# Four tiles in place of two for each step of an expert layer, and a new order of the steps behind the last loads

## The chip, the cores and the metric

The kernel runs on one core of one Trainium2 chip. The metric is the time of one execution in device microseconds. Before the change three runs took 282.29, 282.82 and 283.61 us, the median is 282.82 us.

## The reference

An attention over 49 agents per batch is followed by a soft mixture of experts. Everything is float32, and there are B = 4 batches of N = 11456 tokens with C = 128 channels.

```
a2k  = softmax(scale * agents @ k.T)        agent_v = a2k @ v
q2a  = softmax(scale * q @ agents.T)        x = q2a @ agent_v        (45824 x 128)
logits = x @ phi                            (45824 x 32: 8 experts with 4 slots each)
d = softmax(logits, over the tokens)        slot_input = d.T @ x
slot_out[e] = max(slot_input[e] @ w1[e], 0) @ w2[e]                  (F = 1024)
c = softmax(logits, over the slots)         out = c @ slot_out       (45824 x 128)
```

## The kernel before

The tokens of a batch lie in 90 cells of 128 (four streams of 32), so there are 360 cells. The program is a list of 1281 small steps, each with one engine, the steps that it depends on, and the buffer slots that it takes and gives back. A table of names, `ORDER` (line 49), fixes one order for all of them; each engine then works its own steps off strictly in that order, and the loads and stores are all issued from SP's queue in that order too. The framework adds the semaphore waits, by tile.

The work comes in three stages. The first reads k, v and q in groups of 16 cells, makes the scores on TensorE (`ks`, `qs`, line 243), the softmaxes on VectorE, ScalarE and GpSimd, and the sums of the experts' inputs (`rg`, lines 590 and 598). `x_all` keeps the logits of all cells for the end.

The second stage is the expert layer, between the last sum and the first output. `l4` (line 801) writes the slots' inputs `si`. The hidden layer of 1024 is cut into four quarters, numbered by `fh` (0, 1) and `q` (0, 1). Each quarter is multiplied by w1 (`mh`, line 828, 8 matmuls that the trace shows as 16), rectified (`mr`, line 834 on VectorE for q = 0, line 837 on ScalarE for q = 1), transposed (`mt`, line 844), copied (`mc`, line 848 on ScalarE for q = 0, line 850 on VectorE for q = 1) and multiplied by w2 (`mo`, line 857). The four `mo` add up in one PSUM tile `so_p`; then follow the copy `ms` (line 863), the sum over experts `sb` (868), and `sd` (871), which scales by the tokens' divisor `dr` (`d2` to `d4`, lines 810 to 820) and gives `sob`. Before the change the two quarters of one `fh` share one tile at each step: `hp`, `hs`, `htp` and `ht` have a dimension of two, and each quarter uses its half:

```python
hps[fh] = tile_("s", [P, 2, 512], f"hp_{fh}")      # PSUM, one of three slots "s"
v_.tensor_scalar(out=hss[fh][:, 0, :256], in0=hps[fh][:, 0, :256], ...)      # q = 0
s_.activation(out=hss[fh][:, 1, :256], in_=hps[fh][:, 1, :256], func=AF.Relu)   # q = 1
```

The third stage makes the output in 25 chunks of 4, 4, 8, 8 and then 16 cells. For the cells of each group it takes the logits' maximum (`cr`, line 607, VectorE), subtracts it (`cu`, 611, GpSimd) and takes the exponential (`ce`, 616, ScalarE); for each chunk j it then makes the sum `os` (875, VectorE), the small addition `oe` (879, ScalarE), the reciprocal `or` (882, VectorE), the product `om` (887, GpSimd), the transpose `ot` (893, VectorE), the matmuls with `sob` (`oo`, 901, TensorE, two PSUM buffers), and two copies out of PSUM into one of four output buffers: `va` (911, VectorE, a quarter) and `vb` (914, ScalarE, three quarters). `od` (918) stores it from SP's queue. The steps from `cr` to `ot` can be done long before `sob` is there; where they stand is up to the table. `oo` of chunk 0 is the first that needs `sob`.

The weights are eight loads of 1 MB, `w1` (705) and `w2` (710). `w2` with x = 1, 2, 3 goes into the buffers of q (`qt`), the others into a pool that opens when the last groups of k are done (`ends`, line 925).

Of the kernel before, what the change touches and what calls it, by code (L numbers as in the profile page):

```python
# [100 lines left out]
r412 qv10 ru9.0 re9.0 ru9.1 cu14 r312 rx12 ql11 os1 eh ei qM11 r211 r411 w12 re9.1 ry12.0 r311 or0
cu8 om0 nm os6 rx11 rg9.0 rg12.0 rc12 wt rg9.1 rc9 wr oe1 ry11.0 rg11.0 ry11.1 rg11.1 ws gm qv11
ce10 rc11 l1 l2 w10 f0 ce14 f1 f2 os2 ce11 cu13 l3 l4 oe6 cr19 os4 oe4 dE or1 mh0.0 or3 ot0 mh0.1
mr0.0 om1 cu12 ot1 qv12 w13 mh1.0 os12 os5 mr1.0 cr18 ej mr0.1 ce8 ce12 oe2 om3 mt0.0 mt0.1 mc0.1
mh1.1 mc0.0 mo0 ce15 oe12 mt1.0 or12 or6 oe5 w21 mo1 os7 oe8 or4 os16 or2 cu19 w23 mr1.1 mt1.1
mc1.1 or5 om5 om2 mc1.0 d1 d2 oe7 cr22 cu18 mo2 mo3 ms d3 d4 os13 or7 ce18 oe13 cu22 sb sd oo0 oo1
or8 os17 va0 vb0 om8 od0 ot2 oo2 ot3 ce13 ce17 va1 vb1 od1 os10 va2 om4 vb2 or13 ot4 oo3 va3 om13
om7 om6 vb3 oe10 od3 ot5 cr20 od2 oo4 va4 oo5 ot6 os14 ce19 vb4 od4 ot7 va5 or10 cu20 oe14 cr23
oe9 or9 cu23 om9 vb5 od5 oo6 oo7 va6 ot8 ot9 ce20 os11 vb6 od6 oe11 va7 os15 oe15 or15 om10 oo8
vb7 od7 or14 or11 va8 ot10 om11 oe17 os19 os18 os20 vb8 oo9 va9 oe19 ot11 or19 od8 vb9 od9 om12  # L110
ot12 oo10 va10 vb10 cr21 or17 cr24 cu21 oe16 od10 oo11 va11 ce21 oe20 os22 vb11 od11 om19 ot13
om14 or16 oo12 ot14 oe22 om15 om17 va12 vb12 od12 oo13 oo14 va13 vb13 od13 ot15 va14 oe18 or18
om16 ot16 oo15 ot17 cu24 ce24 vb14 or20 oo16 va15 vb15 od14 om18 ot18 ot19 om20 va16 ot20 ce22
oo17 va17 vb16 od15 vb17 od17 os21 oe21 os23 or22 om22 oo18 va18 vb18 od18 or21 oe23 or23 ce23
os24 oe24 or24 om23 oo19 va19 vb19 od16 od19 oo20 va20 vb20 od20 om21 ot21 oo21 ot22 oo22 ot23
va21 vb21 od21 va22 vb22 od22 oo23 va23 vb23 od23 om24 ot24 oo24 va24 vb24 od24
# [980 lines left out]
```

## Time and profile before

| | |
|---|---|
| runs shown | 282.29, 282.82, 283.61 us (median 282.82) |
| the profiled execution | 284.2 us |
| its span from first to last instruction | 282.3 us |
| busy in the span: TensorE, VectorE, ScalarE, GpSimd | 87%, 78%, 70%, 45% |
| HBM read, written | 79.73 MB, 23.59 MB |
| output stores | 25, of which 21 have 1024 KB |

Times in the profile count from the span's start. "DVE" is VectorE, "ACT" ScalarE, "POOL" GpSimd, "PE" TensorE's matmuls and "PEld" its weight loads, "SPq" the queue from which SyncE issues the transfers. Line numbers are those of the kernel before. A time in square brackets is how long the engine had been idle before the row, with the instruction that ended the wait.

### The profile page before, as it was taken

What the parts mean: (1) busy time and instruction counts of PE and PEld (TensorE: products, weight loads), DVE (VectorE), ACT (ScalarE), POOL (GpSimd) and SP (SyncE); (2) the same over time, 40 slices, a digit from 0 to 9 for tenths busy, and PEclk for the clock granted to TensorE, in tenths of its full rate; (3) what the DMA queues carried; (4) which work ended last, traced back from release to release, by engine and by line L of the source; (5) the groups of instructions that cost most, each with busy time, mean ns of one, the idle gap of its engine ahead of it and who ended that gap; (6) DMA issues with size and microseconds to landing.
All of it is one profiled execution on the core that took longest, in us unless ns stands there. A gap on an engine that the chain in (4) does not pass through costs nothing.

```text
span 282.3 us, 8243 instructions
## 1 busy us (share of the span) xinstructions
PE 244.4 (87%) x3252; PEld 131.4 (47%) x3252; DVE 220.6 (78%) x431; ACT 198.7 (70%) x680; POOL 126.3 (45%) x139
## 2 busy tenths in 40 slices
PE   7959889999999989999999999999987699596810
PEld 4213556642554654455674555777744323131300
DVE  0597774699998977999898999999676999676520
ACT  2559597466997876599798978997643767866540
POOL 0034521207565341474754485994645834725000
PEclk9999999999999999999999999999799987957575
DMA  7999999999999999999999999559900499999995
GB/s 252 425 424 416 419 410 414 423 412 418 346 416 422 416 420 417 407 366 415 419 418 419 421 376 424 201 201 421 414 14 0 193 416 406 411 425 416 423 417 245
DMA packets 16454, 103.86 MB, mean 368 GB/s; under 512 B 2080, under 2 KB 2464, under 8 KB 5152
## 3 DMA queue, kind: packets, MB, share of 16 engines
q1 hardware_dynamic: 16272, 103.25, 89.9%
q8 instruction: 26, 0.43, 0.6%
q10 hardware_dynamic: 144, 0.08, 0.1%
q14 instruction: 12, 0.10, 0.1%
HBM read 79.73 MB, written 23.59 MB: 366 GB/s over the span
## 4 chain that ended last, share of the span: by engine, by line
PE 46%; DMA 32%; DVE 9%; ACT 4%; issue 2%; POOL 2%; SPq 1%; ACTq 0%; DVEq 0%
DMA out<-ot 11%; PE sq L243 11%; PE sk L243 9%; DMA vt<-vL 9%; PE ev L320 8%; DMA kt<-kT 7%; DMA qt<-qT 6%; PE tp L477 5%; PE lq L528 4%; ACT ot L914 3%; PE gp L598 2%; DVE cd L875 2%; PE gp L590 2%; POOL x_all L887 1%; PE so_p L857 1%
## 5 line engine op out<-in xcount | busy, mean ns | idle before, releaser
L445 ACT ACTIVATE pt<-pt,mx 128x49 f32<-128x49 f32 x148 | 47.5, 326 | 0.1
L320 PE MATMUL ev<-vt,et 128*64 128x129 f32 x720 | 44.8, 276 | 3.1 <-DMA vt<-vL 2.7
L243 PE MATMUL sk<-kt,ag 128*32 128x512 f32 (+1 forms) x384 | 45.7, 570 | 1.4 <-DMA kt<-kT 1.1
L243 PE MATMUL sq<-qt,ag 128*32 128x512 f32 (+3 forms) x400 | 43.8, 554 | 3.2 <-DMA qt<-qT 3.0
L320 PEld LDWEIGHTS ev<-vt,et 128*64 128x64 f32 x720 | 39.2, 136 | 10.0 <-issue 6.2
L901 PE MATMUL pa<-ct,sob 32*128 32x512 f32 (+2 forms) x50 | 32.1, 750 | 12.1 <-DVE ct L893 10.1
L466 POOL TENSOR_TENSOR pt<-pt,rt 128x784 f32<-128x784 f32 (+3 forms) x20 | 27.1, 1356 | 33.5 <-DVE rt L462 25.4
L914 ACT COPY ot<-pb 128x1536 f32<-128x1536 f32 (+2 forms) x25 | 32.5, 1306 | 12.7 <-DMA out<-ot 8.1
L303 ACT ACTIVATE es<-sk,nm 128x512 f32<-128x512 f32 (+1 forms) x48 | 29.7, 652 | 10.1 <-DVE nm L294 8.2
L564 POOL TENSOR_TENSOR dt<-x_all,mb 128x512 f32<-128x512 f32 (+1 forms) x20 | 24.2, 1218 | 22.6 <-DVE mb L560 15.1
L887 POOL TENSOR_TENSOR x_all<-x_all,cd 128x512 f32<-128x512 f32 (+2 forms) x25 | 23.5, 961 | 23.1 <-DVE cd L882 18.1
L901 PE MATMUL pb<-ct,sob 32*128 32x512 f32 (+2 forms) x150 | 33.6, 772 | 0.1
L313 DVE STREAM_TRANSPOSE et<-es 128x1024 f32<-128x1024 f32 (+1 forms) x24 | 28.0, 1165 | 3.1 <-ACT es L303 3.1
L611 POOL TENSOR_TENSOR x_all<-x_all,r_all 128x512 f32<-128x512 f32 (+3 forms) x25 | 23.9, 962 | 11.7 <-DVE r_all L607 5.9
L482 ACT COPY pT<-tp 128x1024 f32<-128x1024 f32 (+3 forms) x25 | 22.8, 918 | 8.6 <-PE tp L477 8.6
L275 DVE TENSOR_REDUCE mt<-sk 128x2 f32<-128x1024 f32 (+1 forms) x24 | 27.4, 1140 | 1.8 <-PE sk L243 1.5
L445 ACT ACTIVATION_READ_ACCUMULATOR pt<-pt,mx 128x1 f32 x148 | 28.1, 190 | 0.0
L911 DVE COPY ot<-pa 128x512 f32<-128x512 f32 (+2 forms) x25 | 15.5, 620 | 11.2 <-DMA out<-ot 9.2
L901 PEld LDWEIGHTS pa<-ct,sob 32*128 32x128 f32 x50 | 9.3, 226 | 31.9 <-DVE ct L893 20.2
L420 DVE STREAM_TRANSPOSE pt<-sq 128x1024 f32<-128x1024 f32 (+3 forms) x20 | 21.8, 1095 | 2.0 <-PE sq L243 1.5
L243 PEld LDWEIGHTS sq<-qt,ag 128*32 128x32 f32 x400 | 11.0, 109 | 22.9 <-issue 16.3
L477 PE MATMUL tp<-cs,pt 128*128 128x128 f32 x140 | 21.4, 283 | 0.0
(133 smaller groups left out, 421.4 us busy)
## 6 DMA issues: line engine op xcount, KB each, us to landing
out<-ot SPq DMA_DIRECT2D x21, 1024.0 KB, 7.7
vt<-vL SPq DMA_DIRECT2D x20, 1032.0 KB, 11.5
qt<-qT SPq DMA_DIRECT2D x20, 1024.0 KB, 9.6
kt<-kT SPq DMA_DIRECT2D x19, 1024.0 KB, 9.4
w2s<-w SPq DMA_DIRECT2D x4, 1024.0 KB, 13.5
w1s<-w SPq DMA_DIRECT2D x4, 1024.0 KB, 11.2
vt<-vL SPq DMA_DIRECT2D x4, 645.0 KB, 8.6
kt<-kT SPq DMA_DIRECT2D x4, 640.0 KB, 9.0
```

What stands on the lines that cost most here:

```text
L243: t_.matmul(sp[32 * q4:32 * q4 + 32, h, :nt], ag[:, b, 32 * h:32 * h + 32], xv[:, q4, :], start=True, stop=True)
L275: v_.tensor_reduce(out=k["mt"][:, 0:2], in_=k["s"][:, :, :nt], axis=AX.X, op=ALU.max, negate=True)
L303: s_.activation(out=k["e"][:, h, :nt], in_=k["s"][:, h, :nt], func=AF.Exp, bias=k["nm"][:, 2 * h:2 * h + 1])
L313: v_.transpose(out=k["et"][:, :n].rearrange("p t (h a) -> p h t a", h=2), in_=k["e"][:, :, :nt].rearrange("p h (t a) -> p h t a", a=32))
L320: t_.matmul(k["ev"][o:o + AW, :], k["et"][:, c, :], k["v"][:, c, :], start=c < 2, stop=c >= n - 2)
L445: s_.activation(out=x, in_=x, func=AF.Exp, bias=q["mx"][:, c:c + 1], accum_out=q["rt"][:, c:c + 1])
L466: g_.tensor_tensor(out=x, in0=x, op=ALU.mult, in1=q["rt"][:, :n].unsqueeze(2).to_broadcast([P, n, A]))
L477: t_.transpose(q["tp"][:, h, j % 4, :], q["pt"][:, 2 * j:2 * j + 2, :].rearrange("p c a -> p (c a)"), ident)
L564: g_.tensor_tensor(out=q["dt"][:, :q["n"]], in0=x_all[:, q["at"]:q["at"] + q["n"]], op=ALU.add, in1=r["mb"].unsqueeze(1).to_broadcast([P, ...
L887: g_.tensor_tensor(out=x, in0=x, op=ALU.mult, in1=z["cd", j].unsqueeze(2).to_broadcast([P, n, S]))
L901: t_.matmul(pb[:, r - 1, :32 * n] if r else pa[:, :32 * n], sob[32 * r:32 * r + 32, :], z["ct", j][32 * r:32 * r + 32, :32 * n], start=Tru ...
L914: s_.copy(out=o_ov(j)[:, 1:4], in_=z["pb", j][:, :, :32 * CHUNKS[j]])
```

## The change

Each quarter of the expert layer gets tiles of its own: `hp` and `htp` (PSUM) and `hs` and `ht` (SBUF) are made once for each `fh` and `q`. The steps lose their dependence on the other quarter of the same `fh`, the slots are taken where the tile is written and given back when that one tile is done with, and `mc` takes its own SBUF slot. The first output matmul gets the last transposes of the logits (`qv`) as a further dependence. The table `ORDER` is new from the end of the last k groups on: the same 1281 steps stand in another order there, loads included. No operation is added, and none is removed.

```diff
-qc21 cu16 kv22 kE22 kv23 cu11 kE23 cr14 cr17 cu7 qw24 ka22 qE22.3 ce16 qr24 qr19 ce7 cr15 qr23
+qc21 cu16 kv22 kE22 kv23 cu11 cr14 cu7 qr19 qN19 cr15 kE23 cr12 w21 qE22.3 ka22 qr23 kA22 ce4 kA23
...
     def m_h(fh, q):
-        if q == 0:
-            hps[fh] = tile_("s", [P, 2, 512], f"hp_{fh}")
-            hss[fh] = tile_("pt", [P, 2, 512], f"hs_{fh}")
+        h = hps[fh, q] = tile_("s", [P, 256], f"hp_{fh}{q}")
...
     def m_relu(fh, q):
-        if q == 0:
-            v_.tensor_scalar(out=hss[fh][:, 0, :256], in0=hps[fh][:, 0, :256], scalar1=0.0,
-                             scalar2=None, op0=ALU.max)
+        h = hss[fh, q] = tile_("pt", [P, 256], f"hs_{fh}{q}")
+        if q:
+            s_.activation(out=h, in_=hps[fh, q], func=AF.Relu)
         else:
-            s_.activation(out=hss[fh][:, 1, :256], in_=hps[fh][:, 1, :256], func=AF.Relu)
+            v_.tensor_scalar(out=h, in0=hps[fh, q], scalar1=0.0, scalar2=None, op0=ALU.max)
 
     def m_trans(fh, q):
-        if q == 0:
-            htp[fh] = tile_("s", [P, 2, 4, P], f"htp_{fh}")
-            hts[fh] = tile_("pt", [P, 2, 4, P], f"ht_{fh}")
+        htp[fh, q] = tile_("s", [P, 2, P], f"htp_{fh}{q}")
...
     def m_copy(fh, q):
-        if q == 0:
-            s_.copy(out=hts[fh][:, 0, 0:2], in_=htp[fh][:, 0, 0:2])
+        h = hts[fh, q] = tile_("pt", [P, 2, P], f"ht_{fh}{q}")
+        if q:
+            v_.tensor_copy(out=h, in_=htp[fh, q])
         else:
-            v_.tensor_copy(out=hts[fh][:, 1, 0:2], in_=htp[fh][:, 1, 0:2])
+            s_.copy(out=h, in_=htp[fh, q])
...
+            h = op("mh", (fh, q), "P", lambda fh=fh, q=q: m_h(fh, q),
+                   deps=[si4] + wx[2 * fh:2 * fh + 2], takes=("s",))
+            r = op("mr", (fh, q), "A" if q else "V", lambda fh=fh, q=q: m_relu(fh, q),
+                   deps=(h,), takes=("pt",), gives=(("s", h),))
+            t = op("mt", (fh, q), "P", lambda fh=fh, q=q: m_trans(fh, q), deps=(r,),
+                   takes=("s",), gives=(("pt", r),))
+            c[2 * fh + q] = op("mc", (fh, q), "V" if q else "A", lambda fh=fh, q=q: m_copy(fh, q),
+                               deps=(t,), takes=("pt",), gives=(("s", t),))
...
+    ops["oo", 0]["deps"] += [("qv", ri) for ri in range(NR)]
```

Three places in the order of the instructions show what moves. The first is ScalarE in the expert layer. The steps `mr` (line 837 before, 833 now) and `mc` (848, 847) stand among the exponentials and the small additions; in square brackets is the engine whose semaphore the instruction waits for. Before:

```order
L879 ACTIVATE cd_3090<-cd_3090 128x16 [waits DVE_49]
L837 ACTIVATE hs_3099<-hp_3098 128x256 [waits DVE_49]
L616 ACTIVATE x_all<-x_all 128x512 [waits Pool_49] x2
L879 ACTIVATE cd_3081<-cd_3081 128x8
L848 COPY ht_3149<-htp_3148 128x256 [waits DVE_49]
L616 ACTIVATE x_all<-x_all 128x512
...
L837 ACTIVATE hs_3127<-hp_3126 128x256 [waits PE_49]
L848 COPY ht_3176<-htp_3175 128x256 [waits DVE_49]
```

And with the change:

```order
L876 ACTIVATE cd_3100<-cd_3100 128x16 [waits DVE_49]
L833 ACTIVATE hs_3133<-hp_3124 128x256 [waits PE_49]
L833 ACTIVATE hs_3146<-hp_3137 128x256 [waits PE_49]
L847 COPY ht_3151<-htp_3148 128x256 [waits PE_49]
L616 ACTIVATE x_all<-x_all 128x512
...
L847 COPY ht_3213<-htp_3188 128x256 [waits PE_49]
L616 ACTIVATE x_all<-x_all 128x512
L616 ACTIVATE x_all<-x_all 128x512 [waits Pool_49]
L820 COPY dr<-dr_p 128x1 [waits PE_49]
```

Three of the four instructions waited for VectorE, which had its own half of the same tile to write or read; now all four wait for TensorE alone.

The second place is TensorE in the expert layer (line 826 now was 828, 840 was 844, 854 was 857). Before:

```order
L828 MATMUL hp_3126<-w1s,si 32x256 [waits DMAHW6_49]
L828 MATMUL hp_3126<-w1s,si 32x256 x3
L844 MATMUL htp_3148<-cs,hs_3099 128x128 [waits DVE_49]
L844 MATMUL htp_3148<-cs,hs_3099 128x128
L844 MATMUL htp_3148<-cs,hs_3099 128x128 [waits Activation_49]
L844 MATMUL htp_3148<-cs,hs_3099 128x128
L828 MATMUL hp_3126<-w1s,si 32x256 [waits DVE_49]
L828 MATMUL hp_3126<-w1s,si 32x256 x7
L857 MATMUL so_p<-w2s_2825,ht_3149 32x256 [waits DMAHW2_49,Activation_49]
```

And with the change:

```order
L826 MATMUL hp_3137<-w1s,si 32x256 x3
L840 MATMUL htp_3148<-cs,hs_3116 128x128 [waits DVE_49]
L840 MATMUL htp_3148<-cs,hs_3116 128x128
L751 MATMUL d_p<-cs,gt 32x1
L826 MATMUL hp_3159<-w1s,si 32x256 [waits Activation_49]
L826 MATMUL hp_3159<-w1s,si 32x256 x7
L840 MATMUL htp_3168<-cs,hs_3133 128x128 [waits Activation_49]
L840 MATMUL htp_3168<-cs,hs_3133 128x128
L840 MATMUL htp_3171<-cs,hs_3146 128x128 [waits Activation_49]
L840 MATMUL htp_3171<-cs,hs_3146 128x128
L854 MATMUL so_p<-w2s_2801,ht_3151 32x256 [waits DMAHW7_49,DVE_49]
```

Three products stand ahead of the first transpose in both; the fourth stood behind a wait for VectorE (the half of its own tile that VectorE reads) and now stands behind one transpose and a wait for ScalarE (a PSUM slot given back), and two transposes separate it from the first product with w2.

The third place is VectorE between the copies `va` of chunks 0 and 3 (line 911 before, 908 now). Before:

```order
L911 COPY ot_3273<-pa_3258 128x128
L893 STREAM_TRANSPOSE ct_3278<-x_all 128x256
L893 STREAM_TRANSPOSE ct_3286<-x_all 128x256
L911 COPY ot_3290<-pa_3264 128x128
L875 TENSOR_REDUCE cd_3294<-x_all 128x16
L911 COPY ot_3296<-pa_3280 128x256
L882 RECIPROCAL cd_3238<-cd_3238 128x16
L893 STREAM_TRANSPOSE ct_3301<-x_all 128x512
L911 COPY ot_3309<-pa_3303 128x256
```

And with the change:

```order
L908 COPY ot_3274<-pa_3268 128x128
L890 STREAM_TRANSPOSE ct_3276<-x_all 128x256
L879 RECIPROCAL cd_3079<-cd_3079 128x16
L879 RECIPROCAL cd_3100<-cd_3100 128x16
L908 COPY ot_3291<-pa_3283 128x128
L879 RECIPROCAL cd_2816<-cd_2816 128x16
L890 STREAM_TRANSPOSE ct_3310<-x_all 128x512
L908 COPY ot_3312<-pa_3298 128x256
L890 STREAM_TRANSPOSE ct_3314<-x_all 128x512
L607 TENSOR_REDUCE r_all<-x_all 128x4
L879 RECIPROCAL cd_3233<-cd_3233 128x16
L607 TENSOR_REDUCE r_all<-x_all 128x16
```

One transpose has gone ahead of `sob`, and so has the reduction between the copies of chunks 1 and 2; three reciprocals have come between. On SP's queue the load of `w2` with x = 1, which stood behind the wait for the last k groups, stands ahead of it now, directly behind the last load of v, and needs no wait; six loads of weights are left behind the wait where seven were.

## Rows read from the trace of the kernel before

**Rows 1.** Stretches: us, busy PE, PEld, DVE, ACT, POOL, granted clock, DMA share, GB/s.
```profile
180.00:185.00 5.00, 5.00 (x86) 4.63 (x84) 4.77 (x11) 4.71 (x15) 4.54 (x5) 1.00 0.18 70
...
220.00:225.00 5.00, 3.96 (x32) 1.53 (x32) 4.48 (x12) 4.83 (x9) 4.38 (x6) 1.00 0.53 205
225.00:230.00 5.00, 3.72 (x21) 1.50 (x24) 4.68 (x11) 3.51 (x6) 3.05 (x4) 1.00 1.04 421
230.00:235.00 5.00, 4.90 (x17) 1.50 (x15) 4.72 (x12) 3.32 (x6) 2.33 (x3) 0.51 0.95 392
```
**Rows 2.** Timeline, expert layer: start, us, engine, line, operation, count [idle <-releaser].
```profile
203.48 0.91 DVE L540 STREAM_TRANSPOSE x_all<-lq 128x704 f32<-128x704 f32 x1
205.45 0.18 DVE L801 TENSOR_TENSOR si<-si_p,sie 128x32 f32<-128x32 f32 x1
205.69 2.80 PE L828 MATMUL hp<-w1s,si 128*32 128x256 f32 x48
206.14 0.68 DVE L875 TENSOR_REDUCE cd<-x_all 128x16 f32<-128x512 f32 x1
207.69 0.42 DVE L834 TENSOR_SCALAR hs<-hp 128x256 f32<-128x256 f32 x1 [0.52 <-PE hp L828]
208.15 0.38 ACT L837 ACTIVATE hs<-hp 128x256 f32<-128x256 f32 x1 [1.07 <-DVE hs L834]
208.58 0.66 PE L844 MATMUL htp<-cs,hs 128*128 128x128 f32 x4
210.07 1.07 PE L828 MATMUL hp<-w1s,si 128*32 128x256 f32 x16 [0.83 <-DVE hs L834]
211.03 0.37 ACT L848 COPY ht<-htp 128x256 f32<-128x256 f32 x1 [1.37 <-DVE ht L850]
211.46 1.07 PE L857 MATMUL so_p<-w2s,ht 128*32 128x256 f32 x16 [0.31 <-ACT ht L848]
214.76 0.37 ACT L848 COPY ht<-htp 128x256 f32<-128x256 f32 x1 [2.24 <-DVE ht L850]
215.18 1.93 PE L857 MATMUL so_p<-w2s,ht 128*32 128x256 f32 x32 [0.77 <-ACT ht L848]
217.19 0.42 DVE L863 COPY so<-so_p 128x256 f32<-128x256 f32 x1 [1.25 <-PE so_p L857]
218.49 0.35 DVE L871 TENSOR_SCALAR sob<-sb_p,dr 128x128 f32<-128x128 f32 x1
```
**Rows 3.** Timeline, the first output chunks.
```profile
219.46 0.28 DVE L911 COPY ot<-pa 128x128 f32<-128x128 f32 x1
219.54 0.48 ACT L914 COPY ot<-pb 128x384 f32<-128x384 f32 x1 [1.09 <-PE pb L901]
219.92 0.99 ACT L616 ACTIVATE x_all<-x_all 128x512 f32<-128x512 f32 x2
221.43 0.24 DVE L882 RECIPROCAL cd<-cd 128x16 f32<-128x16 f32 x1
222.96 0.62 ACT L616 ACTIVATE x_all<-x_all 128x512 f32<-128x512 f32 x1
223.57 1.44 ACT L914 COPY ot<-pb 128x1536 f32<-128x1536 f32 x1
223.64 0.68 DVE L911 COPY ot<-pa 128x512 f32<-128x512 f32 x1
225.03 10.12 SPq L918 DMA_DIRECT2D out<-ot  x5
```
**Rows 4.** Timeline, the matmuls of two later chunks, at half clock and at full.
```profile
231.24 2.07 PE L901 MATMUL pa<-ct,sob 32*128 32x512 f32 x2
...
238.00 1.12 PE L901 MATMUL pa<-ct,sob 32*128 32x512 f32 x2
```
**Rows 5.** SP's queue: the last loads of v, the first load behind the wait.
```profile
169.66 8.24 SPq L266 DMA_DIRECT2D vt<-vL  x2
185.59 0.33 SPq L710 DMA_DIRECT2D w2s<-w  x1
```

More of the change, by code (lines that the diff above doesn't have):

```diff
@@ L101 @@
[L101 to L116, printed above, removed]
+qc21 cu16 kv22 kE22 kv23 cu11 cr14 cu7 qr19 qN19 cr15 kE23 cr12 w21 qE22.3 ka22 qr23 kA22 ce4 kA23
+w12 qw24 re8.0 eb cu8 qp18.0 qp18.1 w23 w10 qN23 kg23.1 qw22 kh23.1 qr24 os2 cr13 kg23.2 kh23.2
@@ new lines @@
+os1 qN24 kh23.4 w11 w20 qp19.0 kg23.3 os3 os6 w13 qr22 os8 kh23.3 qp19.1 ql10 qM10 r210 qc18 qc19
+oe6 ec ed qp24.0 qc24 ql9 r410 r310 ce16 oe1 qN22 qp22.0 qM9 qv9 rx10 rg8.0 r29 ry10.0 rg8.1 rc8
+qp22.1 oe2 ry10.1 cu2 ce2 qc22 ef qz24 qp23.0 eg cu15 ce7 ce15 r49 ql12 rg10.0 rg10.1 r39 or2 qM12
+r59 or1 r212 r412 qc23 ql11 ru9.0 rc10 ru9.1 qv10 r312 rx12 re9.0 eh ei qM11 r211 ry12.0 r411 r311
+nm os0 rg9.0 rg12.0 om1 re9.1 rg9.1 rx11 rc12 wt wr oe3 cr20 cu20 cu14 ce11 rc9 f0 ry11.0 rg11.0
+ry11.1 rg11.1 ws gm os5 oe0 rc11 l1 or0 qv12 om0 ce8 oe5 ce14 f1 l2 l3 oe8 cr17 f2 l4 os10 qv11 dE
@@ new lines @@
+mh0.0 mr0.0 oe10 or6 os4 os16 mh0.1 mr0.1 or3 ej mh1.1 mr1.1 mt0.0 mc0.0 ce10 os7 oe7 d1 mh1.0
+mt0.1 mt1.1 mo0 cr22 ot0 mr1.0 mt1.0 oe4 om6 cu17 mc0.1 cu13 ce13 or4 om4 om2 cr21 mc1.1 mo1 ce17
+mc1.0 mo2 mo3 ot1 os17 cu12 ce20 ce12 cr19 ot2 d2 ms os14 d3 or7 sb d4 sd om3 os9 oo0 va0 ot3 cu21
+om7 or5 om5 or10 oo1 vb0 od0 va1 oe9 vb1 or8 om8 od1 oo2 oo3 ot4 va2 ot5 cr24 oe17 om10 or17 vb2
+od2 cr18 va3 oo4 vb3 va4 ot6 ot7 od3 oo5 vb4 od4 or9 om9 cu18 os18 va5 ot8 ce21 vb5 od5 ce9 os12
+oo6 va6 os15 ce18 vb6 od6 ot9 ot10 oe12 cu22 ce22 os23 oe14 or12 om12 oo7 oo8 oe16 va7 vb7 od7 va8
@@ new lines @@
+vb8 od8 or14 om17 om14 oo9 os13 os11 oe11 or11 va9 oo10 va10 vb10 od10 oe23 os22 om11 cu19 or23
+ot11 os19 ot12 ce19 oo11 oe13 or13 om13 om23 os20 oe15 or15 vb9 va11 od9 cu24 om15 vb11 od11 ot13
+oe18 or18 om18 oe19 oo12 ot14 va12 vb12 oe20 or19 oo13 va13 or16 vb13 od13 oo14 ot15 om16 ot16
+ot17 oe22 or22 om22 va14 or20 om20 vb14 od14 oo15 va15 ot18 oo16 om19 vb15 od15 od12 oo17 va16
+vb16 va17 oo18 va18 vb17 od16 ot19 ot20 vb18 od18 oo19 os21 oe21 or21 om21 va19 vb19 ot21 cr23
+cu23 ce23 ce24 od17 oo20 oo21 va21 vb21 od21 va20 os24 oe24 vb20 od20 ot22 or24 om24 ot23 oo22
@@ L117 @@
+va22 ot24 vb22 od22 oo23 va23 od19 vb23 od23 oo24 va24 vb24 od24
 """
@@ L958, in tile_agent_attn_soft_moe @@
     d4 = op("d4", (), "A", z_d4, deps=(d3,), gives=(("a", d3),))
-    h, t, c = {}, {}, {}
+    c = {}
     for fh in range(2):
-        h[fh] = [op("mh", (fh, q), "P", lambda fh=fh, q=q: m_h(fh, q),
-                    deps=[si4] + wx[2 * fh:2 * fh + 2] + ([("mh", fh, 0)] if q else []),
-                    takes=() if q else ("s", "pt")) for q in range(2)]
-        r = [op("mr", (fh, q), "A" if q else "V", lambda fh=fh, q=q: m_relu(fh, q),
-                deps=[h[fh][q]], gives=(("s", h[fh][0]),)) for q in range(2)]
-        t[fh] = [op("mt", (fh, q), "P", lambda fh=fh, q=q: m_trans(fh, q),
-                    deps=[r[q]] + ([("mt", fh, 0)] if q else []),
-                    takes=() if q else ("s", "pt"), gives=(("pt", h[fh][0]),)) for q in range(2)]
-        c[fh] = [op("mc", (fh, q), "V" if q else "A", lambda fh=fh, q=q: m_copy(fh, q),
-                    deps=[t[fh][q]], gives=(("s", t[fh][0]),)) for q in range(2)]
+        for q in range(2):
+            h = op("mh", (fh, q), "P", lambda fh=fh, q=q: m_h(fh, q),
[6 more added lines that the diff above has]
+                               deps=(t,), takes=("pt",), gives=(("s", t),))
     mo = None
@@ L974, in tile_agent_attn_soft_moe @@
         mo = op("mo", (x,), "P", lambda x=x: m_out(x),
-                deps=[c[x // 2][x % 2], wy[x], ("am", 0)] + ([mo] if mo else []),
-                takes=() if x else ("a",), gives=(("pt", t[x // 2][0]),))
+                deps=[c[x], wy[x], ("am", 0)] + ([mo] if mo else []),
+                takes=() if x else ("a",), gives=(("pt", c[x]),))
     ms = op("ms", (), "V", m_so, deps=(mo,), gives=(("a", ("mo", 0)),))
```

10 lines of the change are left out of this document (3 added, 7 removed).

## The prediction

> **What bounds the kernel now.** I read the busy time by stretches first, then the timeline of the expert layer, then that of the first output chunks. The stretches [rows 1] show the kernel bound by transfers at both ends with a hole between: the DMA engines move 421 GB/s at share 1.04 from 225 to 230 us, but 205 GB/s from 220 to 225 us and 70 GB/s from 180 to 185 us. The 23.59 MB of output take 56.0 us at 421 GB/s, and from 220 us to the span's end at 282.3 us there are 62. So the end follows from when the output starts to flow, and what the other engines save after that is worth nothing as long as they keep ahead of the stores. What sets the start is the expert layer [rows 2]: its input `si` is ready at 205.63 us (205.45 plus 0.18) and `sob` at 218.84 us (218.49 plus 0.35), 13.2 us, and no output can start before it. In those rows the reader should look at what stands in the brackets. TensorE waited 0.83 us for VectorE's relu, 0.31 us for ScalarE's copy and 0.77 us for the next one. ScalarE's copies began right after VectorE's copy of the other half of the tile (brackets of 1.37 and 2.24 us, both ended by DVE ht), and its relu behind VectorE's relu (1.07 us). VectorE's first relu came 0.52 us late, at 207.69 us, although its own product was done well before: 48 matmuls took 2.80 us from 205.69 us, so the first quarter's 16 were done about 0.93 us after that.
>
> **The expert layer: minus 1.8 us.** The change gives each quarter its own tiles, and the order of the instructions shows the waits for the other engine's half gone. What remains on TensorE is the work itself. From the first product at 205.69 us to the last w2 product at 217.11 us (215.18 plus 1.93) are 11.42 us, of which the three waits in brackets are 0.83 + 0.31 + 0.77 = 1.91 us. All of it is on the path, so 1.91 us is what there is to gain. Whether new waits come in its place I check step by step, with the times of [rows 2]:
> - Three products end at 205.69 + 2.80 = 208.49 us. VectorE does a reduction (0.68), the last transpose of logits (0.91, it stood ahead of `si` before) and then the relu (0.42) after 205.63 us: done at 207.6 us, before the transpose wants it. The 0.91 us are covered by the three products; without that cover they would be on the path.
> - The fourth product needs a PSUM slot from ScalarE's relu of the third, which ends some 0.45 us after 208.49 us. One transpose (0.66 for four instructions, so 0.33 for two) fills most of that: 0.1 us may show.
> - Two more transposes (0.66) and that product (1.07) bring TensorE to about 210.7 us. ScalarE's first copy, 0.37 us after a transpose that ended near 208.9 us, is long there.
> - VectorE has eight small steps between its two relus, four of them as long as 0.68: at most 2.9 us with 0.42 for the relu itself, done near 210.9 us. Its transpose is wanted after the first w2 product, at 210.7 + 1.07 = 211.8 us. The remaining copies come out 0.6 us or more ahead of their products.
>
> I take 1.91 minus 0.1, so 1.8 us, with 1.4 (the slack of the second relu gone) and 1.9 as ends. Behind the last product nothing changes: copy, sum over experts and scaling keep their 1.7 us.
>
> **The order ahead of the expert layer: plus 0.2 us.** The steps that made chunk sums there are permuted on VectorE, ScalarE and GpSimd, and TensorE's row of instructions is the same up to `si`. VectorE gets a 16-cell reduction (0.68 at most) in place of a 10-cell one and one reciprocal (0.24, [rows 3]) in another place ahead of the last keys' result. I read 0 to 0.4 us of delay on the path from this, and take 0.2, since other steps leave the same stretch. Together the two terms put `sob` at 218.84 minus 1.6, which is 217.2 us.
>
> **The load of w2 that moves: nothing.** SP issued the last load of v at 177.9 us (169.66 plus 8.24) and then stood until 185.59 us at the wait for the last key groups [rows 5], with the DMA engines at 0.18 of their time [rows 1]. One of seven 1 MB loads now goes into that hole, so the weights are all there 2.5 us sooner (1.05 MB at 421 GB/s). No bracket in the expert layer names a weight load, so nobody waited for them: nothing to gain. It passes no wait on SP, and behind it the queue's wait is the same.
>
> **The first chunks: minus 0.6 us.** From the start of the first copy to the end of the fifth, the first of full size, VectorE took 219.46 to 224.32 us and ScalarE 219.54 to 225.00 us [rows 3]; then the fifth store went out at 225.03 us. On ScalarE 0.99 + 0.62 us of exponentials stood between; the new order has two additions there instead, so up to 1.4 us go. On VectorE a full reduction (0.68, [rows 2]) and a half-size transpose give way to three reciprocals (0.72) and a small reduction: 0.1 us less or so by these durations. In the rows it is ScalarE's copy that ends last and sets the store, 0.68 us behind VectorE's. It can start 1.4 us sooner as far as ScalarE goes, but it needs the chunk's product, and that needs VectorE's transposes and copies, 0.1 us sooner. Between the two I take 0.6 us, nearer VectorE's, because every chunk passes it first; the ends for the range are 0 and 1.0.
>
> **The rest of the output: plus 0.3 us.** From 225 us on an earlier start passes to the end in full if the stores never run dry. In the first stretch at half clock (0.51) they moved 392 instead of 421 GB/s, which is 29 x 5 / 421 = 0.35 us lost [rows 1]. Half clock costs a chunk's two matmuls of one quarter 2.07 instead of 1.12 us [rows 4]. I take 0.3 us for a place where the faster start meets unprepared chunks, with 0 and 1.3 (0.35 + 0.95) as ends.
>
> **The sum** is 1.8 - 0.2 + 0.6 - 0.3 = 1.9 us. The profiled execution took 284.2 us with a span of 282.3 us, so it would take 282.3 us. It stands 1.4 us above the median of the runs, 282.82 us; from the median the forecast is **280.9 us**. The ends of the terms alone give 1.4 - 0.4 + 0 - 1.3 = -0.3 and 1.9 - 0 + 1.0 - 0 = 2.9 us of gain, so 283.1 to 279.9 us.
>
> **Rivals.**
> - *The start is given back at half clock.* `sob` comes earlier, but chunks 9 to 14 are prepared later relative to it, since the new order moves the exponentials and reductions of several groups between the output copies. With the clock at half there, one dry spell of 0.95 + 0.35 = 1.3 us follows, and the gain is 1.8 - 0.2 + 0.6 - 1.3 = 0.9 us: 281.9 us. For it speaks the 0.51 of [rows 1]; against it that the DMA engines stayed at 0.95 there. The Trainium skill's page "TensorE: Matmul & The Clock Gate" (Part 1: The HAM clock gate) says that half rate is the default and that activity releases it. The clock of 1.00 through the expert layer and 0.51 after 230 us agree; by that rule the new order gets no better clock among output copies than the old one, and this rival's time would be the likelier.
> - *Slower: the output stage becomes a chain.* VectorE's reciprocal for chunk 23 now stands ahead of the transpose of chunk 11, and it waits for an addition on ScalarE that stands behind the large copy of chunk 10, which waits for the store of chunk 6 to free one of four buffers. Such knots tie the preparation of a chunk to the landing of a store. There are about five (at chunks 6, 7, 11, 13, 21). One costs nothing while at least two stores lie in the queue; with fewer, it costs about one chunk's half-clock step, 0.95 us. All five: 4.8 us against 2.2 us of gain (1.8 - 0.2 + 0.6), 2.6 us slower, 285.4 us. Against it: a copy (1.44), addition, reciprocal (0.24 each), transpose, matmuls (2.07) and copy (1.44) make about 6 us, and two stores and the two that follow last 10.
> - *The load of w2 delays the last v.* It goes out right behind it. If the two share the engines evenly, the last product with v starts up to 2.5 us late, less whatever it waited anyway, and 280.9 becomes at most 283.4 us. The Trainium skill's page "DMA: Bandwidth & Descriptors" (Two DMAs through the same engine are not ordered) says that within a queue descriptors start in order; by that rule v keeps its place and the price is nothing. No row here shows the case, the two not having stood next to each other.
> - *The waits stay*, as waits for a PSUM slot or for a slot of `pt` that other steps hold: then only 0.1 us is left (-0.2 + 0.6 - 0.3), 282.7 us. Against it: the waits in the new order name TensorE where they named VectorE.
>
> **How the numbers follow.** The forecast gets 0.60, the half-clock rival 0.24, slower by the chain 0.07, the delayed v 0.04, waits that stay 0.05. A measurement of this kernel can tell about 0.5% from no change, so 1.4 us: faster means below 281.4, slower above 284.2 us. Of the forecast's 0.60 I count 0.53 below 281.4 and of the half-clock case 0.08, 0.61 in all; the chain is slower, 0.07; the rest, 0.32, is the same. The range goes from 279.2 us (the best end with a little less idle DMA) to 283.1 us, which holds all but the chain and the worst of the delayed v.
>
> **What would show it.** Right: three of the brackets on TensorE between the first product and the last w2 product gone or below 0.2 us; ScalarE's relu and copies ended by PE; `sob` near 217.2 us; the fifth store out near 222.8 us; DMA share at 1 from there. The half-clock rival shows a stretch between 230 and 250 us under 400 GB/s. Wrong would be: `si` later than 206.3 us, a bracket on the fourth product above 0.5 us, or two or more stretches of the output stage below 380 GB/s.

## The result, and the profile after the change

The kernel with the change took **279.75 us** (median of four runs, 279.15 to 280.75) against 282.81 us before; the ratio is 0.988 with a 95% interval of 0.984 to 0.992. The forecast was 280.9 us, with a range of 279.2 to 283.1, and faster as the likeliest sign. Timed twice more, later and beside other kernels, the change had 0.991 (0.987 to 0.994) and 0.989 (0.984 to 0.993). Medians and ratios here and below are of the fast runs: two runs of the change (284.45 and 283.36 us) and five of before, each over 1.5% above the fastest of its kernel, are left out.

The profiled execution took 279.15 us, with a span of 277.3 us; TensorE is busy in 86% of it, VectorE in 79%, ScalarE in 72%, GpSimd in 46%.

The profile after, on the expert layer, the first chunks and the loads ahead of them (timeline; start, us, engine, line, operation; lines are those of the changed kernel). It answers to [rows 2], [rows 3] and [rows 5]:

```profile
167.83 8.24 SPq L266 DMA_DIRECT2D vt<-vL  x2
176.12 0.42 SPq L710 DMA_DIRECT2D w2s<-w  x1
...
202.50 0.19 DVE L801 TENSOR_TENSOR si<-si_p,sie 128x32 f32<-128x32 f32 x1
202.75 2.80 PE L826 MATMUL hp<-w1s,si 128*32 128x256 f32 x48
204.03 0.39 DVE L835 TENSOR_SCALAR hs<-hp 128x256 f32<-128x256 f32 x1
204.75 0.38 ACT L833 ACTIVATE hs<-hp 128x256 f32<-128x256 f32 x1 [1.21 <-PE hp L826]
205.48 0.44 PE L840 MATMUL htp<-cs,hs 128*128 128x128 f32 x2
205.62 0.38 ACT L833 ACTIVATE hs<-hp 128x256 f32<-128x256 f32 x1 [0.48 <-PE hp L826]
205.85 0.22 PE L751 MATMUL d_p<-cs,gt 50*32 50x1 f32 x2
206.00 1.07 PE L826 MATMUL hp<-w1s,si 128*32 128x256 f32 x16
207.00 0.66 PE L840 MATMUL htp<-cs,hs 128*128 128x128 f32 x4
207.58 1.07 PE L854 MATMUL so_p<-w2s,ht 128*32 128x256 f32 x16
208.59 0.44 PE L840 MATMUL htp<-cs,hs 128*128 128x128 f32 x2
208.95 2.80 PE L854 MATMUL so_p<-w2s,ht 128*32 128x256 f32 x48
209.06 0.37 ACT L847 COPY ht<-htp 128x256 f32<-128x256 f32 x1 [0.64 <-PE htp L840]
213.12 0.35 DVE L868 TENSOR_SCALAR sob<-sb_p,dr 128x128 f32<-128x128 f32 x1
...
216.17 0.69 PE L898 MATMUL pa<-ct,sob 32*128 32x512 f32 x1 [0.32 <-DVE ot L908]
217.50 1.44 ACT L911 COPY ot<-pb 128x1536 f32<-128x1536 f32 x1 [0.59 <-PE pb L898]
218.97 0.33 SPq L915 DMA_DIRECT2D out<-ot  x1
```

The three brackets that TensorE had in [rows 2] are gone. Its rows follow each other from 202.75 to 211.75 us, 9.00 us where there were 11.42. ScalarE's brackets name PE now, where they named DVE. From the end of `si` to the end of `sob` are 10.8 us instead of 13.2. The last row is the fifth store, issued 5.5 us after the end of `sob` instead of 6.2.

The stretches of the changed kernel, answering to [rows 1] (us, busy PE, PEld, DVE, ACT, POOL, granted clock, DMA share, GB/s):

```profile
180.00:185.00 5.00, 4.95 (x69) 4.37 (x68) 4.70 (x12) 4.99 (x19) 4.78 (x5) 1.00 0.43 163
215.00:220.00 5.00, 4.04 (x39) 1.34 (x32) 5.00 (x14) 4.20 (x7) 3.02 (x4) 1.00 0.78 309
220.00:225.00 5.00, 3.55 (x20) 0.91 (x16) 4.93 (x9) 4.30 (x9) 3.01 (x3) 1.00 1.03 419
230.00:235.00 5.00, 2.48 (x16) 0.99 (x16) 4.64 (x11) 4.19 (x7) 1.85 (x3) 0.79 1.01 416
255.00:257.50 2.50, 1.74 (x8) 0.16 (x4) 0.85 (x2) 1.23 (x3) 0.31 (x1) 0.64 1.01 419
257.50:260.00 2.50, 0.79 (x8) 0.40 (x9) 2.36 (x5) 2.21 (x3) 0.64 (x1) 1.00 0.45 187
```

In these two profiles the stores run full some 5 us sooner, and the dip at 230 us is gone. The last row is new: the transfers run dry late, at 187 GB/s, which costs (421 - 187) x 2.5 / 421 = 1.4 us.

The two profiled spans differ by 5.0 us (282.3 and 277.3), the medians by 3.06. So I cut every profile of this study at four instants and read the pieces, which compare far better than whole spans. "v to si" goes from the end of the issue of the last load of v to the end of `si`. Times in us:

| kernel | time (runs) | ratio to before | v issued | v to si | si to sob | sob to 5th store | 5th store to span's end | half clock ahead of si |
|---|---|---|---|---|---|---|---|---|
| before | 282.81 (4) | 1 | 177.9 | 27.7 | 13.2 | 6.2 | 57.3 | yes |
| the change | 279.75 (4) | 0.988 | 176.1 | 26.6 | 10.8 | 5.5 | 58.3 | no |
| the change, again | 279.93 (11) | 0.991 | 177.1 | 28.0 | 10.8 | 5.5 | 57.4 | yes |
| the change, third | 280.12 (5) | 0.989 | 178.4 | 28.0 | 10.8 | 5.5 | 57.3 | yes |
| tiles alone | 281.84 (12) | 0.996 | 177.5 | 26.3 | 11.7 | 6.2 | 57.4 | no |
| order alone | 281.90 (12) | 0.995 | 178.2 | 26.6 | 11.8 | 6.7 | 57.5 | no |
| load of w2 put back | 280.06 (12) | 0.991 | 177.0 | 26.6 | 10.9 | 5.5 | 58.3 | no |
| old order up to si | 279.93 (6) | 0.989 | 177.8 | 26.3 | 11.0 | 5.5 | 58.2 | no |
| old order from the output on | 286.00 (6) | 1.011 | 178.4 | 26.6 | 12.5 | 11.2 | 56.6 | no |
| stores in turn | 279.32 (6) | 0.990 | 176.9 | 26.6 | 10.8 | 5.5 | 56.9 | no |
| stores in turn, again | 279.53 (6) | 0.988 | 177.4 | 26.6 | 10.8 | 5.5 | 56.9 | no |
| stores in turn, old order up to si | 280.56 (8) | 0.992 | 177.5 | 27.7 | 10.9 | 5.5 | 56.9 | yes |
| hp shared | 280.56 (1) | | 176.6 | 26.6 | 11.7 | 5.5 | 58.3 | no |
| tiles alone, slots swapped | 279.00 (1) | | 176.1 | 26.3 | 11.2 | 6.2 | 57.4 | no |

The instant at which v was issued lies anywhere from 176.1 to 178.4 us, with the old order as with the new. It is chance, and 1.8 of the 5.0 us between the two profiled spans are that. What lies behind it repeats within 0.1 us from profile to profile where the same steps run, but for two things that the last columns show: a stretch of half clock, and where the stores run dry. The times of single runs, (1), serve only for their profiles.

### The profile page after: what moved, and what is told of

It is laid out like the page before. It is cut to its first block, busy times and chain, and to the rows that moved or that the text cites. A ratio compares the mean times of both kernels' runs of the same rounds, so it can differ in the third digit from the quotient of the medians.

```text
span 277.3 us, 8239 instructions
## 1 busy us (share of the span) xinstructions
PE 238.8 (86%) x3252; PEld 129.0 (47%) x3252; DVE 220.1 (79%) x431; ACT 198.9 (72%) x680; POOL 126.4 (46%) x139
## 4 chain that ended last, share of the span: by engine, by line
PE 55%; DMA 26%; DVE 9%; ACT 3%; issue 2%; POOL 1%; SPq 1%; DVEq 0%; ACTq 0%
PE sq L243 12%; PE sk L243 11%; PE ev L320 10%; DMA out<-ot 9%; DMA kt<-kT 8%; DMA qt<-qT 6%; PE tp L477 5%; DMA vt<-vL 4%; PE lq L528 4%; PE pa L898 3%; PE gp L598 2%; ACT ot L911 2%; PE so_p L854 1%; PE hp L826 1%; DVE r_all L607 1%
## 5 line engine op out<-in xcount | busy, mean ns | idle before, releaser
L898 PE MATMUL pa<-ct,sob 32*128 32x512 f32 (+2 forms) x50 | 33.5, 790 | 13.9 <-DVE ct L890 7.9
## 6 DMA issues: line engine op xcount, KB each, us to landing
vt<-vL SPq DMA_DIRECT2D x20, 1032.0 KB, 11.2
```

Source lines behind the costliest of these rows:

```text
L898: t_.matmul(pb[:, r - 1, :32 * n] if r else pa[:, :32 * n], sob[32 * r:32 * r + 32, :], z["ct", j][32 * r:32 * r + 32, :32 * n], start=Tru ...
```

## The experiments

**The two halves of the change, each alone.** The first kernel has the new tiles and the table of before; the second the new table and the shared tiles, where the quarter that comes first makes the tile:

```diff
     def m_h(fh, q):
-        if q == 0:
+        if q == fh:
...
```

> The tiles of each quarter are the change's; every step stands in the order of before. Theory A (the expert layer's gain comes from the tiles): from the end of si to the end of sob 11.3 to 11.6 us where before had 13.2 and the change 10.8, since three waits of 1.91 us in all go and what the new order adds is missing; no wait of TensorE over 0.4 us between the first product and the last w2 product; the output stage is that of before, so the time is 282.8 minus 1.7, 281.1 us (280.4 to 281.8), ratio 0.994. Theory B (the order did it, the tiles only allow it): si to sob stays at 12.7 us or more, time 282.3 us or more, ratio 0.998 to 1.002. On the clock: if the stretch at half clock ahead of si belongs to the old order, this run shows one between the last transposes of q and si and si comes 1.4 us later behind the last dt; if it is chance, either may be seen.

> The new order with the old shared tiles (for fh = 1 the quarter that now comes first makes the tile). Theory A: the waits for the other engine's half come back in the new order, si to sob 12.6 us or more (before 13.2, the change 10.8), the ends of 0.6 us of the first chunks stay, and the time is 281.5 to 282.8 us, ratio 0.995 to 1.000. Theory B: si to sob at most 11.6 us and the time at most 280.8 us, ratio 0.993 or less. On the clock: no stretch at half clock ahead of si if the new order is what keeps the clock up; else either.

Tiles alone: 281.84 us, 0.996 (0.993 to 0.999). Order alone: 281.90 us, 0.995 (0.992 to 0.998). Each gives about half. From si to sob the tiles alone take 1.5 us off and the order alone 1.4, both together 2.4. So neither theory held: the tiles are not all of it, and the order works without them too. TensorE with the tiles alone (timeline):

```profile
203.85 2.92 PE L825 MATMUL hp<-w1s,si 128*32 128x256 f32 x48
206.69 0.44 PE L839 MATMUL htp<-cs,hs 128*128 128x128 f32 x2
207.72 0.41 PE L839 MATMUL htp<-cs,hs 128*128 128x128 f32 x2 [0.59 <-ACT ht L846]
```

And with the order alone (TensorE, then ScalarE):

```profile
204.84 1.07 PE L827 MATMUL hp<-w1s,si 128*32 128x256 f32 x16
206.57 1.93 PE L827 MATMUL hp<-w1s,si 128*32 128x256 f32 x32 [0.65 <-DVE hs L833]
...
212.53 0.37 ACT L847 COPY ht<-htp 128x256 f32<-128x256 f32 x1 [1.63 <-DVE ht L849]
```

With the old order one wait of 0.59 us is left although no tile is shared. With the new order one of 0.65 us is left because a tile is shared: the second product would write the tile from which VectorE still reads the first. ScalarE's copy is held up by 1.63 us in the same way, and no bracket of TensorE comes of it; its last 48 products take 2.93 us there and 2.80 in the change. The two kernels below take these two waits apart.

**One tile shared again, `hp`**, in the change:

```diff
-        h = hps[fh, q] = tile_("s", [P, 256], f"hp_{fh}{q}")
+        if q == fh:
+            hps[fh] = tile_("s", [P, 2, 512], f"hp_{fh}")
+        h = hps[fh, q] = hps[fh][:, q, :256]
...
```

> The change with one tile shared again: the two products of one fh write one PSUM tile hp, everything else stays split. With the new order and all tiles shared, si to sob took 11.8 us where the change takes 10.8, and TensorE's only bracket was 0.65 us in front of the second product, ended by VectorE's first relu; ScalarE's second copy began 1.63 us late behind VectorE's but no bracket of TensorE names it. Theory F (the price of sharing is paid at hp alone): that bracket is back, 0.6 to 0.7 us, with 0.2 us of restart, and si to sob is 11.5 to 11.7 us. Theory G (hs, htp and ht cost as much, hidden in the chain of copies): si to sob 11.0 to 11.3 us.

```profile
203.27 1.07 PE L828 MATMUL hp<-w1s,si 128*32 128x256 f32 x16
205.00 1.93 PE L828 MATMUL hp<-w1s,si 128*32 128x256 f32 x32 [0.65 <-DVE hs L837]
```

The bracket is back to the hundredth, and si to sob is 11.7 us: 0.9 us for one shared tile, 0.65 in the bracket and most of the rest in stopping and starting again. In the new order, splitting `hs`, `htp` and `ht` is worth the 0.1 us that is left to the order alone (11.8). Theory F holds.

**Tiles alone, with two PSUM slots swapped.** In the table of before one name moves; no engine's instructions change their order, since the two steps run on different engines:

```diff
-mh1.0 os12 os5 mr1.0 cr18 ej mr0.1
+mh1.0 os12 os5 mr0.1 mr1.0 cr18 ej
```

> The split tiles in the order of before, with one name moved in the table: ScalarE's relu of the second quarter stands ahead of VectorE's relu of the third. No engine's instructions change their order; only the PSUM slots change hands, so that the second pair of transposes takes the slot that ScalarE gave back at 206.24 us and not the one that VectorE gave back at 207.58 us. With the split tiles alone TensorE stood 0.59 us ahead of that pair. Theory (the slot of VectorE's relu is what it waited for): the pair runs on behind the first, the wait goes to the fourth product, which needs the late slot now and starts about 0.4 us sooner than before; si to sob 11.2 to 11.4 us. Rival (the profile names ScalarE's copy as what ended that wait, and it is): bracket and 11.7 us stay.

```profile
205.29 0.66 PE L839 MATMUL htp<-cs,hs 128*128 128x128 f32 x4
206.23 1.07 PE L825 MATMUL hp<-w1s,si 128*32 128x256 f32 x16 [0.28 <-DVE hs L834]
```

All four transposes run on, 0.28 us of the 0.59 remain and stand ahead of the fourth product, and si to sob falls from 11.7 to 11.2 us. So the wait was for the slot of VectorE's relu, which ended at 207.58 us with the tiles alone, although the profile named ScalarE's copy, which ended at 207.63 us. This is part of what the new order does inside the expert layer: it puts the relus where their slots come back in time.

**The load of w2 back behind the wait** (in the table `w21` moves behind `w12`).

> The change with one thing undone: the load of w2 for x = 1 stands behind the wait for the last k groups again, behind w2 for x = 2's neighbour w1, as one of seven loads. Prediction's step (worth nothing): time that of the change, 279.8 us, ratio 0.988 (0.985 to 0.991); the last weight lands near 205 us, 2.5 us later than with the change, still ahead of its product; the last load of v lands within 0.2 us of the same delay after its issue (4.6 us). Rival (the early weights let TensorE go on without a wait): a bracket on a product that names a weight load, time up by 1 us or more, ratio 0.992 or more.

The time is that of the change: 280.06 us, 0.991 (0.988 to 0.994). Yet the load is not quite without effect. The last weight landed 28.9 us after v was issued where the change has 26.4, and TensorE's weight loads show it (timeline of this kernel):

```profile
205.95 0.16 PEld L825 LDWEIGHTS hp<-w1s,si 128*32 128x32 f32 x8 [0.37 <-DMA w1s<-w]
```

It is worth the 0.1 us by which si to sob is longer. In the profile of before nobody waited for a weight, since `si` came 1.4 us late there for another reason, the next point.

**The clock ahead of `si`, and the old order up to there.** Before, TensorE ran at half clock while it made the last sums. The stretches in the profile of before (columns as above), in that of the change, and in the change's second profile:

```profile
199.00:201.00 2.00, 2.00 (x26) 1.74 (x26) 1.12 (x6) 1.15 (x2) 2.00 (x4) 0.60 1.00 410
201.00:203.00 2.00, 2.00 (x26) 1.64 (x18) 0.92 (x2) 0.62 (x4) 1.01 (x2) 0.54 0.98 406
```
```profile
199.00:201.00 2.00, 1.97 (x67) 1.69 (x66) 1.88 (x5) 1.47 (x9) 1.89 (x2) 1.00 0.70 291
201.00:203.00 2.00, 1.92 (x31) 1.59 (x33) 1.58 (x8) 1.34 (x5) 0.56 (x2) 1.00 0.08 29
```
```profile
199.00:201.00 2.00, 2.00 (x34) 1.65 (x34) 1.70 (x5) 1.55 (x5) 0.84 (x1) 0.62 1.01 414
201.00:203.00 2.00, 2.00 (x54) 1.75 (x52) 1.09 (x3) 0.69 (x4) 1.21 (x2) 0.53 0.23 94
```

> The change itself once more, on the same chip as the next three, as their yardstick. From the end of si to the end of sob 10.8 us; si 26.6 us after the last load of v is issued; 62.8 us from the end of sob to the last landing, with the dry place where the store of chunk 19 waits behind later ones. Theory C1 (the half clock ahead of si belongs to the old order): no stretch at half clock ahead of si here; C2 (chance): one may be seen. Time 279.8 to 280.3 us, ratio 0.988 to 0.991.

> The change, but every step up to si's last one stands as before, loads included; what is left follows in the new order. By the profiles the new order ahead of si costs 0.3 us (si 26.6 us after the last load of v is issued, 26.3 with the old order at full clock, 27.7 before the change with 3.4 us at half clock). Theory C1 (the old order draws the half clock in most executions): 0.3 us won and 1.4 lost in most runs, time 0.6 to 1.1 us over that of the change. Theory C2 (chance, the same for both orders): 0.3 us under it. si to sob 10.8 us, or 11.1 if VectorE's work that moves behind si gets in the way.

The half clock comes and goes with the same kernel (the change has it in two of three profiles), so it does not belong to the old order. It costs 1.4 us from v to si (28.0 against 26.6 with the new order, 27.7 against 26.3 with the old), and it shows in 2 of 9 profiles with the new order ahead of `si` and in 2 of 5 with the old, of which before is one; whether the old order meets it more often, so few profiles can't tell. TensorE's work ahead of it is the same in all 14: busy throughout from 14 to 20 us after v is issued, and 76% of the time from 20 to 22 us. In four the granted clock falls to 0.5 between 21 and 23 us, in ten it stays at 1.00. The kernel with the old order up to `si` took 279.93 us, 0.989 (0.985 to 0.993), where theory C1 wanted 0.6 to 1.1 us more than the change's 279.93. Its profile also prices the new order there: 0.3 us from v to si. But the old order does not keep that gain, for there `si` is early and the weights are late (timeline of the kernel with the old order up to `si`):

```profile
206.61 0.16 PEld L825 LDWEIGHTS hp<-w1s,si 128*32 128x32 f32 x8 [0.44 <-DMA w1s<-w]
```

si to sob is 11.0 us in that kernel, so 0.3 us is won ahead of `si` and nearly all of it lost behind. Of the loss, some 0.17 us is the wait for the weight. The other 0.09 us is VectorE's work, as I had it: the third product waits for the slot that VectorE's last transpose of logits gives back, and does so too in the kernel further down that joins the old order with the stores in turn, where no weight is late.

**The stores of chunks 12, 17 and 19 in turn.** In the change's table the stores `od12`, `od17` and `od19` stand behind later stores. Here they stand directly behind their copies:

```diff
-va12 vb12 oe20 ... va19 vb19 ot21 ... va23 od19 vb23 od23
+va12 vb12 od12 oe20 ... va19 vb19 od19 ot21 ... va23 vb23 od23
```

> The change with three stores issued at their chunk's copy: those of chunks 12, 17 and 19 stand directly behind their own copy vb, not behind later stores. In the change's profile chunk 19 was copied by 254.60 us and its store stood in SP's queue behind those of chunks 20 to 23, while the DMA engines ran dry from 256 to 260 us (344 and 209 GB/s). Theory D (the order of the stores made the dry place): 256 to 260 us at 400 GB/s or more, time down by 77 + 212 GB/s over 2 us each at 421 GB/s, 1.4 us, to 278.4 us, ratio 0.984 (0.982 to 0.986). Theory E (the chunk that comes late, 21, sets it, and buffers are the limit, so that a store issued early only moves the dry place): 279.4 to 280 us, ratio 0.987 to 0.990.

What it is about, in the profile of the change (timeline):

```profile
253.16 1.44 ACT L911 COPY ot<-pb 128x1536 f32<-128x1536 f32 x1 [0.83 <-PE pb L898]
...
256.84 1.44 ACT L911 COPY ot<-pb 128x1536 f32<-128x1536 f32 x1 [0.93 <-ACT x_all L616]
...
258.30 3.94 SPq L915 DMA_DIRECT2D out<-ot  x3
```

Chunk 19 was complete at 254.60 us (the first row's end). Its store stood in SP's queue behind those of chunks 21, 20 and 22, and the first of these went out at 258.30 us, so a finished chunk lay by while the DMA engines ran dry. With the stores in turn the same stretch:

```profile
257.50:260.00 2.50, 0.11 (x3) 0.00 (x0) 2.50 (x5) 2.05 (x3) 0.00 (x0) 0.94 1.02 426
```

426 GB/s instead of 187, and 56.9 us from the fifth store to the span's end instead of 58.3. In the profile theory D holds; the time was 279.32 us, 0.990 (0.985 to 0.995), above what D expected. I ran it again beside the change:

> The change with the stores of chunks 12, 17 and 19 issued behind their own copies, again, beside the change on the same chip. From the issue of the fifth store to the last landing 55.9 us (seen in two profiles), where the change had 57.3, 56.4, 57.2 and 57.3 in four profiles with its order of stores. If that gain of 0.5 to 1.4 us is in every execution, the median lies 0.5 to 1.4 us under that of the change in the next run. Rival: the dry place falls where the clock is at half, and that differs from execution to execution, so the medians differ by 0.3 us or less.

> The change itself, as the yardstick of the run before it: 279.8 to 280.3 us, ratio 0.988 to 0.991, si to sob 10.8 us, fifth store 5.5 us after sob, 56.4 to 57.3 us from there to the last landing.

279.53 us, 0.988 (0.984 to 0.992), beside 280.12 us, 0.989 (0.984 to 0.993), for the change. The piece behind the fifth store is 56.9 us in all three profiles with the stores in turn. With the change's order it is 58.2 or 58.3 in the profiles without the early half clock and 57.3 or 57.4 in the two with it, where chunks and clock fall otherwise (the order alone, with granted clock 0.50 from 219.1 to 221.6 us, has its loss among the first chunks, 6.7 us from sob to the fifth store, and 57.5 behind). So the mend is worth 0.4 to 1.4 us by the profile. The times do not settle it: the medians are 0.4 us (279.32 against the first 279.75, which were not timed together) and 0.6 us lower, but the ratios are 0.990 against 0.988 in the first case and 0.988 against 0.989 in the second, all well within their intervals. Which of the three stores matters was not tried.

**Stores in turn and the old order up to `si` together.**

> The change with the old order ahead of si (as in the run with the old front) and with the stores of chunks 12, 17 and 19 issued behind their own copies. If the terms add: 0.3 us from the front and 1.4 us from the stores, 1.7 us under the time of the change, ratio 0.984 or less; by theory C1 on the clock 1.1 of it is lost again. If the stores' gain in the earlier profile was luck of one execution: within 0.5 us of the run with the old front.

280.56 us, 0.992 (0.988 to 0.997): not the 1.7 us. The stores' gain is there in its profile (56.9 us), the 0.3 us of the front is not, for it fell on the half clock (27.7). From the kernel with the old front alone it cannot be told.

**The old order from the first output on.**

> The change up to the first output matmul, and from there every step in the order of before. My step on the first chunks (the new order is worth 0.6 us there, from fewer exponentials between the copies): the fifth store is issued 6.1 us after sob where the change has 5.5. My step on the rest (the new order loses 0.3 us later): no dry place at chunks 19 to 21, 418 GB/s or more from 25 to 55 us behind sob. By the profiles so far the two cancel: sob to the last landing 62.5 us where the change has 62.8, time that of the change within 0.5 us. Rival (the steps that had been done ahead leave the old tail with less work, so both gains come): 61.5 us and a time 1 us or more under the change.

A miss: 286.00 us, 1.011 (1.006 to 1.016), the only kernel here slower than before, and not a test of what I meant. Thirteen steps which the old table has ahead of the first output stand behind it in the new one, so in this mixture they all come between `sob` (at 217.49 us) and the first copies (timeline, VectorE and ScalarE):

```profile
217.41 1.27 DVE L871 TENSOR_REDUCE cd<-x_all 128x16 f32<-128x512 f32 x2
218.59 0.68 DVE L606 TENSOR_REDUCE r_all<-x_all 128x16 f32<-128x512 f32 x1
...
220.16 0.23 DVE L907 COPY ot<-pa 128x128 f32<-128x128 f32 x1
...
221.71 0.63 ACT L615 ACTIVATE x_all<-x_all 128x512 f32<-128x512 f32 x1 [2.78 <-POOL x_all L610]
...
222.35 0.84 ACT L910 COPY ot<-pb 128x384 f32<-128x384 f32 x2
```

VectorE's first copy comes 2.7 us after `sob`, ScalarE's 4.9 us, behind an exponential that waits for GpSimd; the fifth store goes out 11.2 us after `sob` instead of 5.5, and most of the 6 us by which the time is over the change's come from that. It shows in the large what the change does there in the small: steps between `sob` and the first copies put off the fifth store. (Its 12.5 us from si to sob are a half clock in the first products, 4.48 us for the 48.)

## Why the prediction was right, point by point

**The sum.** The forecast was 1.9 us of gain; the medians say 3.06, then 2.79 and 2.95. By the pieces of the profiles the change wins 1.8 us where TensorE keeps its clock ahead of `si` in both kernels (26.3 + 13.2 + 6.2 + 57.3 = 103.0 against 26.6 + 10.8 + 5.5 + 58.3 = 101.2; the 26.3 is from the kernels with the old order there) and 2.7 where it does not (27.7 + 13.2 + 6.2 + 57.3 = 104.4 against 28.0 + 10.8 + 5.5 + 57.4 = 101.7). In the first case the sum comes out right by luck, since 0.6 us too little in the expert layer and 0.7 us too little loss in the rest of the output cancel. The intervals of the ratios reach down to 2.3, 1.6 and 2.0 us, so 1.9 us is likely too little. The measured 279.75 us is also below the best end of the terms, 279.9 us; it lies in the range only for the 0.7 us that the prediction put below that end for "a little less idle DMA" and did not work out. What the medians show above 1.8 to 2.7 us stays open: I have one profile of before, and how often it meets the half clock is not known. The two instants forecast, `sob` at 217.2 and the fifth store at 222.8 us, came at 213.47 and 218.97 us; of these 3.7 to 3.8 us, 1.8 are the earlier issue of v and 1.3 the stretch from v to si, for the clock, neither of them the change's doing.

**The expert layer, minus 1.8 us forecast: 2.4 measured**, outside the ends I gave (1.4 to 1.9). The waits went as predicted, so the mechanism was right. Two things in the step were not. The first is the term "three waits in brackets, 1.91 us, is what there is to gain": it leaves out 0.5 us (11.42 - 9.00 - 1.91). A group of 16 products lasts 1.07 us where TensorE then waits; where it goes on with another kind of work, that starts 1.00 us after the group, and where it goes on with products of the same kind, 0.87 us (2.80 us for three groups). So the three stops cost 0.07 or 0.08 us each beside their brackets, and one change of kind more in the old order 0.13. The other 0.16 us stood ahead of the first transposes (2.89 us after the first product, 2.73 in the change), most of it a wait too short for a bracket. In the kernel with `hp` shared the stop falls between products of one kind and costs 0.20: a bracket of 0.65, a price of 0.9. The second is the cause. I gave the whole term to the tiles; they bring 1.5 us alone, and the new order takes the last 0.9 (11.7 to 10.8), 0.4 of it by slots that come back in time. With the order there first, it is the tiles that take the last 1.0 (11.8 to 10.8). In [rows 2] only brackets on tiles showed, since the slots' wait had no time to show behind them. Of the steps worked out there, the fourth product's slot was sized right: ScalarE's relu was to end 3.25 us after the first product's start, and did, at 206.00 us, when the product started. The "at most 2.9 us" between VectorE's two relus was summed too low: four steps of 0.68 and the relu's 0.42 alone make 3.14, and 3.14 us it took, from 204.42 to 207.56 us. The slack covered it, for the transpose of the second relu began at 208.59 us.

**The order ahead of the expert layer, plus 0.2 us forecast: 0.3 measured** (26.6 against 26.3), in all profiles without the half clock.

**The load of w2, nothing forecast: 0.1 us measured**, far under what a time can tell. The step that failed, in the small, is "no bracket names a weight load": the cover that I read was a `si` made late by half clock in that one execution. The last load of v landed 4.6 us after its issue in the change's profile and with the load put back. Over all profiles it took 4.0 to 5.6 us with the load right behind it and 4.1 to 4.8 without, and in the profile with 5.6 us `si` came 26.6 us after v as ever, so the rival in which it is delayed by up to 2.5 us is out. The Trainium skill's page "DMA: Bandwidth & Descriptors" (Two DMAs through the same engine are not ordered) says that within a queue descriptors start in order, and by this v keeps its place; the trace agrees. The two loads had stood next to each other before, though the prediction says not: SP issued a load of w2 at 166.71 us right behind one of v at 166.24 us, and v landed at 174.97, w2 at 177.65 us.

**The first chunks, minus 0.6 us forecast: 0.7 measured** (6.2 to 5.5). As the step said, ScalarE's exponentials no longer set the store: its fifth copy now waits 0.59 us for TensorE's product, which itself waited 0.32 us for VectorE's copy. The old tail shows the same place at its worst.

**The rest of the output, plus 0.3 us forecast: 0.0 to 1.0 measured** (57.3 before; 57.3 to 58.3 in the profiles with the change's output order). It is one dry place, as the step said, but late chunks at half clock do not make it alone: with the stores in turn the clock is as low there (0.50 from 250 to 257.5 us), and the stores do not run dry. A finished chunk's store stood behind unfinished ones. I had read the order of the copies and not that of the stores, though the table shows it.

**The rivals.** The start given back at half clock was half right: up to 1.0 us was given back, at 258 us instead of between 230 and 250. The chain through the stores did not come about; the DMA share is 1 until 257 us. The waits did not stay. The prediction took from the Trainium skill's page "TensorE: Matmul & The Clock Gate" (Part 1: The HAM clock gate), by which half rate is the default and activity releases it, that the new order gets no better clock among output copies. The trace agrees (mean granted clock from `sob` to the span's end 0.73 after, 0.72 before), but the loss that I had tied to it did not come where I looked for it.

## To carry to other kernels

A wait on TensorE cost its bracket and 0.07 to 0.20 us more here, and behind a wait for a shared tile the next one, for a slot of a pool, doesn't show until the first is gone: after splitting tiles, look at the order in which slots come back. In a queue that issues in order, a store belongs behind its own copy, not behind a later chunk's; here that is shown by the profiles and not by the times. And with programs whose executions differ by more than the effect, cut the profile at fixed instants: pieces that met no stretch of half clock repeated within 0.1 us, where whole spans of the change differed by 2.7.
